# A causal convolution as 32x32 diagonal products, with the loop around it in a new order

## The chip, the cores and the metric

The kernel runs on one core of one Trainium2 chip. What counts is the device time of one execution in microseconds. Engines are named as in the profile: PE is TensorE (PEld its weight loads), DVE is VectorE, ACT is ScalarE, POOL is GpSimd, SP issues DMAs.

## What is computed

Causal linear attention with a decay per head, then a gated linear unit whose gate is a causal convolution of five taps, each channel by itself:

```python
# q, k, v: (8, 8, 576, 64); w_val, w_out: (512, 512); conv_w: (5, 512)
scores = q @ k.T / sqrt(64)
Dmat[h, i, j] = gamma[h] ** (i - j) if i >= j else 0
x = ((scores * Dmat) @ v).transpose(0, 2, 1, 3).reshape(8, 576, 512)
gate_pre[:, s, d] = sum(conv_w[t, d] * xp[:, s + t, d] for t in range(5))  # xp: x with 4 zero rows ahead
out = (sigmoid(gate_pre) * (x @ w_val)) @ w_out
```

## The kernel before

The sequence of each batch is cut into two units of 256 positions and a tail of 64. Sixteen full units come first (0 to 15); the tails of four batches make one unit each (16 and 17). The decay is factored: `gin` is multiplied into v, `gout` into the result, and a mask handles the diagonal blocks. What lies before a block of 128 comes in through a running state.

For one unit `n` these steps are issued, and every engine takes its own in the order in which they stand in the program (the schedule is written out by hand; the pools only say when a buffer is free):

- `load` issues the DMAs of k, q and v on SP's queue, five units ahead; `cast` makes bf16 of them on POOL (k, q, then v with the decay).
- `turn` transposes k and q on PE into the PSUM tile `a`; `take_turn` copies them, in two halves, to SBUF on ACT (`kq`, L249).
- `scores(n, 0)` and `scores(n, 1)` are 64x64 products into the PSUM tile `s` (L266), each half followed by `masks` on DVE (`p`, L276).
- `carried` multiplies the state into the output banks `o0` and `o1` (L307); `values` adds p times v there (L330).
- `take_x` brings the two output banks to SBUF as `xg`, the activations x, on DVE (L341; L348 for the tail).
- `update` makes the state's increment for the next unit in the tile `s` (L367); ACT copies it to `xf` (L375), and POOL adds it up (L380 to L392).
- `conv(n - 1, 0)` is the convolution of the unit before, as products with diagonal matrices `dg` (L424); `gates` takes the sigmoid on ACT (L433).
- `gate_values` multiplies x by w_val in two parts (L445), each followed by the product with the gate on DVE (`z`, L452).
- `rows_out` projects by w_out (L461), copies the two results on ACT (`ob`, L464) and stores them on SP's queue.

The eight PSUM banks are shared out to four pools of two banks each: `psa` (tile `a`: transposes, convolution), `pss` (tile `s`: scores and the state's update), `pso` (`o0`, `o1`) and `psv` (tile `v`: values of w_val and projections, two buffers of one bank). The tile `s` has one buffer, so scores wait until masks or `xf` have read what was there.

Before the loop the first four units are handled in a written-out lead-in, with loads and constants; the loop runs from unit 4 to 17. In it the order is: scores 0 and masks, convolution of n - 1, carried states woven into scores 1, masks, `gate_values`, `values`, `take_x`, `update(n + 1)`, `cast(n + 2)`, `turn(n + 1)`, `rows_out(n - 1)`. After the loop come the convolution, values and projections of unit 17.

In the convolution the channels of x stand in four blocks of 128 partitions. A 64x64 product takes one half of the partitions to one half of the output's, and a diagonal weight on 64 columns does one tap for 64 channels; four such products (two halves in, two halves out) go to two banks.

Of the kernel before, what the change touches and what calls it, by code (L numbers as in the profile page):

```python
# [13 lines left out]
F32 = mybir.dt.float32  # L14
BF16 = mybir.dt.bfloat16
AF = mybir.ActivationFunctionType
ALU = mybir.AluOpType
# [4 lines left out]
def kernel(  # L22
# [10 lines left out]
    nc = tc.nc  # L33
    B, H, S, D = q.shape
    DM = moe_w_val.shape[0]
    KC = moe_conv_w.shape[0]
    P = 128
    NP = H // 2
# [11 lines left out]
    consts = ctx.enter_context(tc.tile_pool(name="c", bufs=1))  # L50
# [5 lines left out]
    gp = ctx.enter_context(tc.tile_pool(name="gp", bufs=1))  # L56
    zp = ctx.enter_context(tc.tile_pool(name="zp", bufs=2))
# [3 lines left out]
    small = ctx.enter_context(tc.tile_pool(name="small", bufs=1))  # L61
    ps_a = ctx.enter_context(tc.tile_pool(name="psa", bufs=1, space=PSUM))
    ps_s = ctx.enter_context(tc.tile_pool(name="pss", bufs=1, space=PSUM))
    ps_o = ctx.enter_context(tc.tile_pool(name="pso", bufs=1, space=PSUM))
# [6 lines left out]
    NU = len(units)  # L71

    jobs = [(u,) for u in range(NU)]
    lo, hi = slice(0, 64), slice(64, 128)
# [3 lines left out]
    with tc.manual_schedule():  # L78
# [26 lines left out]
        wvf = consts.tile([P, NP, DM], F32, name="wvf")  # L105
        wof = consts.tile([P, NP, DM], F32, name="wof")
        load(1)
        nc.sync.dma_start(out=wvf, in_=moe_w_val.rearrange("(o i) n -> i o n", i=P))
        wo_src = moe_w_out.rearrange("(pr ab hl p) n -> ab hl p pr n", pr=2, ab=2, hl=2)
        for (p0, blk, ab, hl) in ((0, 0, 0, 0), (64, 0, 1, 0), (0, 2, 1, 1), (64, 2, 0, 1)):  # L110
            nc.sync.dma_start(out=wof[p0:p0 + 64, blk:blk + 2, :], in_=wo_src[ab, hl])
        for u in range(2, 5):
            load(u)

# [13 lines left out]
        nc.vector.tensor_copy(identf, ident[0:32, 0:32])  # L128
        id2 = small.tile([P, 64], F32, name="id2")
        nc.vector.tensor_tensor(id2, ident[:, 0:64], ident[:, 64:128], op=ALU.add)  # L130

        posi = small.tile([P, S], mybir.dt.int32, name="posi")
        for c in range(2 * NC2):
# [46 lines left out]

        wvb = consts.tile([P, NP, NP, P], BF16, name="wvb")
        wob = consts.tile([P, NP, DM], BF16, name="wob")
        dg = consts.tile([P, NP, KC, 64], BF16, name="dg")

        def prep_conv():
            cps = ps_a.tile([P, KC * NP], F32, name="a")
            nc.tensor.transpose(cps, cwn, identf[0:KC * NP, 0:KC * NP])
            cw = small.tile([P, KC * NP], F32, name="cw")
            nc.vector.tensor_copy(cw, cps)
            nc.vector.tensor_tensor(  # L190
                dg.rearrange("p o k j -> p k o j"),
                cw.rearrange("p (k o) -> p k o", o=NP).unsqueeze(3).to_broadcast([P, KC, NP, 64]),
                id2.unsqueeze(1).unsqueeze(1).to_broadcast([P, KC, NP, 64]), op=ALU.mult)

        def prep_wv():
            src = wvf.rearrange("p o (pr ab hl j) -> p o pr ab hl j", pr=2, ab=2, hl=2)
            for (i, (blk, j0, ab, hl)) in enumerate(((0, 0, 0, 0), (0, 64, 1, 0), (2, 0, 1, 1), (2, 64, 0, 1))):
                nc.scalar.copy(wvb[:, :, blk:blk + 2, j0:j0 + 64], src[:, :, :, ab, hl, :])

        def prep_wo():  # L200
            for o in range(NP):
# [29 lines left out]
        def turn(u, pool, parts=(0, 1)):  # L231

            if u not in kqt:
                kqt[u] = [tp_sb.tile([P, 2, 2, 2, 2, 64], BF16, name=f"kq{hf}") for hf in range(2)]
            if pool is ps_a:
                tps[u] = pool.tile([P, 2, 2, 2, 2, P], BF16, name="a")
            for i in parts:
                if pool is ps_a:
                    ps = tps[u][:, i]
                else:  # L240
                    ps = tps[u, i] = pool.tile([P, 2, 2, 2, P], BF16, name="v" if pool is ps_v else f"o{i}")
                for hf in range(2):
                    for prl in range(2):
                        for r in range(2):
                            h = 2 * (2 * hf + prl)
                            nc.tensor.transpose(ps[:, hf, prl, r, :], bf[u]["kq"[i]][:, r, h:h + 2, :].rearrange("p h d -> p (h d)"), ident)  # L246

        def take_turn(u, hf):
            nc.scalar.copy(kqt[u][hf].rearrange("p i l r c a -> p i (l r c a)"),  # L249
                           tps[u][:, :, hf].rearrange("p i l r a -> p i (l r a)"))  # L250
# [43 lines left out]
        def carried(u, odd, chs=(0, 1)):  # L294

            kind, b, cu = units[u]
            o = out_banks(u)
            for pr in range(NP):
                t = kqt[u][pr // 2]
                for c in chs:  # L300
                    par = c ^ odd
                    rows = half[par]
                    if kind == "full":
                        st = state.get((b, 2 * cu + c))
                        if st is None:
                            continue
                        nc.tensor.matmul(o[c][rows, pr, :], lhsT=st[rows, pr, :],  # L307
                                         rhs=t[rows, 1, pr % 2, :, c, :],
                                         start=first(u, c, par), stop=False, skip_group_check=True)
                    else:  # L310
                        for i in range(2):
                            st = state[b + 2 * c + i, 4]
                            cs = slice(i * 32, i * 32 + 32)
                            nc.tensor.matmul(o[c][rows, pr, :].rearrange("p (r a) -> p r a", r=2)[:, :, cs],
                                             lhsT=st[rows, pr, :], rhs=t[rows, 1, pr % 2, :, c, cs],
                                             start=first(u, c, par), stop=False, skip_group_check=True)
# [80 lines left out]
        def width(j):  # L397
            return W * len(jobs[j])

        def xs(j, rows, blk, shift):  # L400
            kind, b, c = units[jobs[j][0]]
            if kind == "full":
                c0 = c * W + shift
                return xg[rows, b, blk, c0:c0 + width(j)]
            c0 = NC2 * W + shift
            return xg[rows, b:b + GB * len(jobs[j]), blk, c0:c0 + TAIL]

        gsb, zsb = {}, {}
# [3 lines left out]
        def sets(j, i):  # L412
            return (0, 1) if len(jobs[j]) == 1 else (i,)
# [1 line left out]
        cps = {}  # L415

        def conv(j, i, gate=True):
            n, ss = width(j), sets(j, i)
            g = ps_a.tile([P, 2, len(ss), n], F32, name="a")
            for si, s in enumerate(ss):  # L420
                a, b = 2 * s, 2 * s + 1
                for kk in range(KC):
                    for (rows, blk, cols, bank) in ((lo, a, lo, 0), (hi, b, lo, 1), (lo, b, hi, 0), (hi, a, hi, 1)):
                        nc.tensor.matmul(g[cols, bank, si, :], lhsT=dg[rows, blk, kk, :], rhs=xs(j, rows, blk, kk),  # L424
                                         start=(si == 0 and kk == 0), stop=(si == len(ss) - 1 and kk == KC - 1),
                                         skip_group_check=True)
            cps[j, i] = g
            if gate:
                gates(j, i)

        def gates(j, i):
            t = gp.tile([P, 2, len(sets(j, i)), width(j)], F32, name="gate")
            nc.scalar.activation(t, cps[j, i], AF.Sigmoid)  # L433
            gsb[j, i] = t
            if i == 0:
                zsb[j] = zp.tile([P, NP, width(j)], BF16, name="z")

        vps = {}

# [9 lines left out]

        def gated(j, i, e):  # L450
            ss = sets(j, i)
            nc.vector.tensor_tensor(zsb[j][:, 2 * e + ss[0]:2 * e + ss[-1] + 1, :], gsb[j, i][:, e], vps[j, i, e], op=ALU.mult)  # L452

        outs = {}

# [22 lines left out]
        def gate_values(n, e):  # L478
            value(n, 0, e)
            gated(n, 0, e)  # L480

        def rows_out(n):
            project(n, 0, 0)
            project(n, 0, 1)
            store(n)
# [124 lines left out]
        for n in range(4, NU):  # L610
            if n + 5 < NU:
                load(n + 5)
            scores(n, 0)
            masks(n, 0)
            conv(n - 1, 0)
            carried(n, 0)
            scores(n, 1, lambda: carried(n, 1))
            masks(n, 1)
            for e in range(2):
                gate_values(n - 1, e)  # L620
            values(n, 1)
            values(n, 0)
            take_x(n)
            if n + 1 < NU:
                update(n + 1)
                if n + 2 < NU:
                    cast(n + 2)
                turn(n + 1, ps_a)
                take_turn(n + 1, 0)
                take_turn(n + 1, 1)  # L630
            rows_out(n - 1)
        conv(NU - 1, 0)
        for e in range(2):
            gate_values(NU - 1, e)
# [31 lines left out]
```

## Time and profile before

| | |
|---|---|
| two timed runs | 166.9 and 169.79 us, median 168.34 |
| span of the profiled execution | 169.3 us |
| mean granted TensorE clock | 0.969 |
| PE / DVE / ACT / POOL busy | 150.8 / 99.6 / 88.8 / 98.4 us |
| DMA | 40.35 MB, 238 GB/s in the mean |
| instruction queue of PE (q8) | 26 packets, 0.43 MB |

No other time of the profiled execution than its span is on record. In a group's line stand the source line, engine, operation, tiles written and read, shapes and count; then the busy time and the mean nanoseconds of one, and the engine's idle time before them with what ended it. In the chain and the timelines a line has a start and a length in microseconds from the start of the span.

### The profile page before, as it was taken

To read this page: it belongs to the slowest core of one execution; us is meant where nothing else is said; L and a number is where in the kernel's file an instruction comes from. 1 tells how busy PE (TensorE), PEld (TensorE's weight loads), DVE (VectorE), ACT (ScalarE), POOL (GpSimd) and SP (SyncE) were. 2 spreads that over 40 slices of the span, in tenths; PEclk is the share of its full clock that TensorE was granted. 3 is DMA by queue.
4 is the path that set the end of the run, shared out by engine and by line. 5 is a ranking of instruction groups with operands and counts; after the bars stand their busy time and mean duration, and the time that the engine had idled before them with its cause. 6 is when DMAs were issued, how large, how long until landed. Compare 5 with 4: busy or idle time off the path is not lost.

```text
span 169.3 us, 7640 instructions
## 1 busy us (share of the span) xinstructions
PE 150.8 (89%) x3384; PEld 112.8 (67%) x3402; DVE 99.6 (59%) x153; ACT 88.8 (52%) x127; POOL 98.4 (58%) x123
## 2 busy tenths in 40 slices
PE   6677589978899979998999999999999999999960
PEld 2366456647678756877787776868787877868620
DVE  5684543475758481858383856658584938668330
ACT  6965330565273827382838374564838382654520
POOL 7565197157875846584849594956769499100000
PEclk9999755999999999999999999999999999999999
DMA  4999978999999999999999999787980311303125
GB/s 143 290 341 351 284 218 258 316 325 322 314 323 329 282 342 295 307 332 323 329 282 327 296 304 274 251 235 237 240 273 21 128 68 60 127 9 128 45 78 126
DMA packets 61071, 40.35 MB, mean 238 GB/s; under 512 B 2394, under 2 KB 57710, under 8 KB 61038
## 3 DMA queue, kind: packets, MB, share of 16 engines
q1 hardware_dynamic: 61008, 39.86, 77.7%
q8 instruction: 26, 0.43, 1.1%
q14 instruction: 7, 0.06, 0.1%
q10 hardware_dynamic: 30, 0.01, 0.0%
HBM read 30.42 MB, written 9.44 MB: 235 GB/s over the span
## 4 chain that ended last, share of the span: by engine, by line
PE 77%; DMA 5%; DVE 4%; issue 4%; POOL 4%; ACT 2%; SPq 1%; POOLq 0%; ACTq 0%; DVEq 0%
PE v L445 18%; PE v L461 17%; PE a L424 13%; PE a L246 8%; PE s L266 6%; PE o L330 6%; PE o L307 3%; DMA fqc<-in_q_dram 3%; PE s L367 2%; POOL vb L215 2%; DMA fkc<-in_k_dram 2%; DVE p L276 2%; SPq L90 1%; PE o L246 1%; DVE z L452 1%
## 5 line engine op out<-in xcount | busy, mean ns | idle before, releaser
L276 DVE TENSOR_TENSOR p<-s,mask 128x1024 bf16<-128x1024 f32 x28 | 34.3, 1224 | 40.2 <-PE s L266 40.2
L445 PE MATMUL v<-xg,wvb 128*128 128x256 bf16 x288 | 36.6, 281 | 0.5 <-DVE xg L341 0.5
L215 POOL TENSOR_TENSOR vb<-fvc,gin 128x1024 bf16<-128x1024 f32 x18 | 34.3, 1903 | 3.3 <-DMA fvc<-in_v_dram 3.3
L461 PE MATMUL v<-wob,z 128*128 128x512 bf16 x126 | 33.5, 380 | 1.3 <-DVE z L452 0.4
L249 ACT COPY kq<-a 128x1024 bf16<-128x1024 bf16 x28 | 27.0, 1015 | 10.0 <-PE a L246 10.0
L445 PEld LDWEIGHTS <-wvb 128*128 128x128 bf16 x288 | 27.3, 100 | 6.4 <-issue 1.4
L452 DVE TENSOR_TENSOR z<-gate,v 128x512 bf16<-128x512 f32 x36 | 24.6, 683 | 9.2 <-ACT gate L433 5.3
L433 ACT ACTIVATE gate<-a 128x1024 f32<-128x1024 f32 x18 | 18.4, 1024 | 16.1 <-PE a L424 9.1
L464 ACT COPY ob<-v 128x512 f32<-128x512 f32 x36 | 20.0, 605 | 9.6 <-PE v L461 9.6
L424 PE MATMUL a<-xg,dg 64*64 64x256 bf16 x720 | 24.2, 278 | 0.0
L375 ACT COPY xf<-s 128x512 f32<-128x512 f32 x12 | 7.0, 586 | 31.2 <-PE s L367 31.2
L341 DVE TENSOR_TENSOR xg<-o,gout 128x512 bf16<-128x512 f32 x32 | 22.2, 741 | 0.2
L461 PEld LDWEIGHTS <-z 128*128 128x128 bf16 x144 | 13.0, 98 | 13.6 <-DVE z L452 1.4
L424 PEld LDWEIGHTS <-dg 64*64 64x64 bf16 x720 | 20.5, 109 | 2.1 <-DVE xg L348 0.4
L266 PEld LDWEIGHTS <-kq 64*64 64x64 bf16 x576 | 13.5, 106 | 11.0 <-issue 10.0
L266 PE MATMUL s<-kq 64*64 64x128 bf16 x512 | 16.5, 223 | 3.2 <-issue 2.8
L389 POOL TENSOR_TENSOR mid<-run,xf 128x256 f32<-128x256 f32 x8 | 5.8, 727 | 20.3 <-ACT xf L375 14.2
L221 POOL CAST kb<-fkc 128x1024 bf16<-128x1024 f32 x16 | 16.6, 1039 | 0.2 <-DMA fkc<-in_k_dram 0.2
L221 POOL CAST qb<-fqc 128x1024 bf16<-128x1024 f32 x15 | 15.6, 1041 | 0.2 <-DMA fqc<-in_q_dram 0.2
L380 POOL CAST s<-xf 128x256 bf16<-128x256 f32 x8 | 3.2, 398 | 20.2 <-ACT xf L375 13.6
L330 PE MATMUL o<-p,vb 64*64 64x128 bf16 x576 | 12.6, 224 | 1.2 <-DVE p L276 1.2
L330 PEld LDWEIGHTS <-vb 64*64 64x64 bf16 x576 | 9.4, 109 | 5.3 <-issue 5.1
(75 smaller groups left out, 157.7 us busy)
## 6 DMA issues: line engine op xcount, KB each, us to landing
fkc<-in_k_dram SPq DMA_DIRECT2D x32, 256.0 KB, 5.1
fqc<-in_q_dram SPq DMA_DIRECT2D x32, 256.0 KB, 5.1
fvc<-in_v_dram SPq DMA_DIRECT2D x32, 256.0 KB, 5.1
out_dram<-ob SPq DMA_DIRECT2D x16, 512.0 KB, 4.8
wvf<-in_moe_w_val_dram SPq DMA_DIRECT2D x1, 1024.0 KB, 9.2
wof<-in_moe_w_out_dram SPq DMA_DIRECT2D x4, 256.0 KB, 10.0
fkc<-in_k_dram SPq DMA_DIRECT2D x8, 128.0 KB, 4.1
fqc<-in_q_dram SPq DMA_DIRECT2D x8, 128.0 KB, 4.5
```

The lines of the kernel that those rows point to most:

```text
L215: nc.gpsimd.tensor_tensor(t.rearrange("p h r d -> p (h r) d"), loaded["v", u].rearrange("p h (r d) -> p (h r) d", r=2), gin[:, units[u][2] ...
L221: (eng or nc.gpsimd.tensor_copy)(t.rearrange("p r h d -> p h r d"), loaded[n, u].rearrange("p h (r d) -> p h r d", r=2))
L249: nc.scalar.copy(kqt[u][hf].rearrange("p i l r c a -> p i (l r c a)"), tps[u][:, :, hf].rearrange("p i l r a -> p i (l r a)"))
L266: nc.tensor.matmul(s[half[c], par, prl, r, :], lhsT=t[half[par], 0, prl, r, c, :], rhs=t[half[par], 1, prl, :, c, :], start=True, stop=Tru ...
L276: nc.vector.tensor_tensor(p.rearrange("p e l r a -> p (e l) (r a)"), sps[u, hf].rearrange("p e l r a -> p (e l) (r a)"), m.rearrange("p r ...
L330: nc.tensor.matmul(o[c][half[par], pr, :], lhsT=vb[half[c], 2 * pr + par, r, :], rhs=p[half[c], par, prl, r, :], start=first(u, c, par), s ...
L341: nc.vector.tensor_tensor(x[:, b, :, PAD + i0:PAD + i0 + P].rearrange("p o (a r) -> p o r a", r=2), o[c].rearrange("p o (r a) -> p o r a", ...
L424: nc.tensor.matmul(g[cols, bank, si, :], lhsT=dg[rows, blk, kk, :], rhs=xs(j, rows, blk, kk), start=(si == 0 and kk == 0), stop=(si == len ...
L445: nc.tensor.matmul(vp[:, si, :], lhsT=wvb[:, o, 2 * e + s, :], rhs=xs(j, slice(0, P), o, PAD), start=(si == 0 and o == 0), stop=(si == len ...
L452: nc.vector.tensor_tensor(zsb[j][:, 2 * e + ss[0]:2 * e + ss[-1] + 1, :], gsb[j, i][:, e], vps[j, i, e], op=ALU.mult)
L461: nc.tensor.matmul(o, lhsT=z[:, r, :], rhs=wob[:, jj, :], start=(jj == 0), stop=(jj == NP - 1))
L464: (eng or nc.scalar.copy)(outs[u][:, r], o)
```

## The change

Three things. The convolution uses products of 32x32: sixteen per tap (four quarters of the partitions in, four quarters out), one bank for each quarter in, so that it takes four banks, the two of `a` and the two of `o0` and `o1`. The sigmoid is taken bank by bank. So that x's channels meet the right gate, the columns of w_val and the rows of w_out are laid out in another order. And the loop has `gate_values` right after the convolution, and `turn(n + 1)` and `rows_out(n - 1)` before `values`, `take_x`, `update` and `cast`.

```diff
-        wo_src = moe_w_out.rearrange("(pr ab hl p) n -> ab hl p pr n", pr=2, ab=2, hl=2)
-        for (p0, blk, ab, hl) in ((0, 0, 0, 0), (64, 0, 1, 0), (0, 2, 1, 1), (64, 2, 0, 1)):
-            nc.sync.dma_start(out=wof[p0:p0 + 64, blk:blk + 2, :], in_=wo_src[ab, hl])
+        wo_src = moe_w_out.rearrange("(j i p) n -> j p i n", j=4, i=4)
+        for j in range(4):
+            nc.sync.dma_start(out=wof[32 * j:32 * j + 32], in_=wo_src[j])
...
+        id4 = small.tile([P, 32], F32, name="id4")
+        nc.vector.tensor_tensor(id4, id2[:, 0:32], id2[:, 32:64], op=ALU.add)
...
-        dg = consts.tile([P, NP, KC, 64], BF16, name="dg")
+        dg = consts.tile([P, NP, KC, 32], BF16, name="dg")
...
-            src = wvf.rearrange("p o (pr ab hl j) -> p o pr ab hl j", pr=2, ab=2, hl=2)
-            for (i, (blk, j0, ab, hl)) in enumerate(((0, 0, 0, 0), (0, 64, 1, 0), (2, 0, 1, 1), (2, 64, 0, 1))):
-                nc.scalar.copy(wvb[:, :, blk:blk + 2, j0:j0 + 64], src[:, :, :, ab, hl, :])
+            src = wvf.rearrange("p o (j i c) -> p o j i c", j=4, i=4)
+            for i in range(4):
+                nc.scalar.copy(wvb[:, :, i].rearrange("p o (j c) -> p o j c", j=4), src[:, :, :, i, :])
...
         def conv(j, i, gate=True):
-            n, ss = width(j), sets(j, i)
-            g = ps_a.tile([P, 2, len(ss), n], F32, name="a")
-            for si, s in enumerate(ss):
-                a, b = 2 * s, 2 * s + 1
-                for kk in range(KC):
-                    for (rows, blk, cols, bank) in ((lo, a, lo, 0), (hi, b, lo, 1), (lo, b, hi, 0), (hi, a, hi, 1)):
-                        nc.tensor.matmul(g[cols, bank, si, :], lhsT=dg[rows, blk, kk, :], rhs=xs(j, rows, blk, kk),
-                                         start=(si == 0 and kk == 0), stop=(si == len(ss) - 1 and kk == KC - 1),
-                                         skip_group_check=True)
-            cps[j, i] = g
-            if gate:
-                gates(j, i)
+            n = width(j)
+            g = ps_a.tile([P, 2, 512], F32, name="a")
+            go = [ps_o.tile([P, 512], F32, name=f"o{c}") for c in range(2)]
+            bank = [g[:, 0], g[:, 1], go[0], go[1]]
+            for kk in range(KC):
+                for d in range(4):
+                    for rg in range(4):
+                        cg = (rg + d) % 4
+                        rows, cols = slice(32 * rg, 32 * rg + 32), slice(32 * cg, 32 * cg + 32)
+                        nc.tensor.matmul(bank[rg][cols, 0:n], lhsT=dg[rows, cg, kk, :], rhs=xs(j, rows, cg, kk),
+                                         start=(kk == 0), stop=(kk == KC - 1), skip_group_check=True)
+            cps[j, i] = (g, go)
+            gates(j, i)
...
-            t = gp.tile([P, 2, len(sets(j, i)), width(j)], F32, name="gate")
-            nc.scalar.activation(t, cps[j, i], AF.Sigmoid)
+            n = width(j)
+            t = gp.tile([P, NP, n], F32, name="gate")
+            g, go = cps[j, i]
+            for c in range(2):
+                nc.scalar.activation(t[:, 2 + c], go[c][:, 0:n], AF.Sigmoid)
+            nc.scalar.activation(t[:, 0:2], g[:, :, 0:n], AF.Sigmoid)
...
             conv(n - 1, 0)
+            for e in range(2):
+                gate_values(n - 1, e)
             carried(n, 0)
             scores(n, 1, lambda: carried(n, 1))
             masks(n, 1)
-            for e in range(2):
-                gate_values(n - 1, e)
+            if n + 1 < NU:
+                turn(n + 1, ps_a)
+                take_turn(n + 1, 0)
+                take_turn(n + 1, 1)
+            rows_out(n - 1)
             values(n, 1)
             values(n, 0)
             take_x(n)
...
                 update(n + 1)
                 if n + 2 < NU:
                     cast(n + 2)
-                turn(n + 1, ps_a)
-                take_turn(n + 1, 0)
-                take_turn(n + 1, 1)
-            rows_out(n - 1)
```

More of the change, by code (lines that the diff above doesn't have):

```diff
@@ L191, in prep_conv @@
                 dg.rearrange("p o k j -> p k o j"),
-                cw.rearrange("p (k o) -> p k o", o=NP).unsqueeze(3).to_broadcast([P, KC, NP, 64]),
-                id2.unsqueeze(1).unsqueeze(1).to_broadcast([P, KC, NP, 64]), op=ALU.mult)
+                cw.rearrange("p (k o) -> p k o", o=NP).unsqueeze(3).to_broadcast([P, KC, NP, 32]),
+                id4.unsqueeze(1).unsqueeze(1).to_broadcast([P, KC, NP, 32]), op=ALU.mult)
         def prep_wv():
-            src = wvf.rearrange("p o (pr ab hl j) -> p o pr ab hl j", pr=2, ab=2, hl=2)
-            for (i, (blk, j0, ab, hl)) in enumerate(((0, 0, 0, 0), (0, 64, 1, 0), (2, 0, 1, 1), (2, 64, 0, 1))):
-                nc.scalar.copy(wvb[:, :, blk:blk + 2, j0:j0 + 64], src[:, :, :, ab, hl, :])
+            src = wvf.rearrange("p o (j i c) -> p o j i c", j=4, i=4)
+            for i in range(4):
+                nc.scalar.copy(wvb[:, :, i].rearrange("p o (j c) -> p o j c", j=4), src[:, :, :, i, :])
         def prep_wo():
@@ L417, in conv @@
         def conv(j, i, gate=True):
-            n, ss = width(j), sets(j, i)
-            g = ps_a.tile([P, 2, len(ss), n], F32, name="a")
-            for si, s in enumerate(ss):
-                a, b = 2 * s, 2 * s + 1
-                for kk in range(KC):
-                    for (rows, blk, cols, bank) in ((lo, a, lo, 0), (hi, b, lo, 1), (lo, b, hi, 0), (hi, a, hi, 1)):
-                        nc.tensor.matmul(g[cols, bank, si, :], lhsT=dg[rows, blk, kk, :], rhs=xs(j, rows, blk, kk),
-                                         start=(si == 0 and kk == 0), stop=(si == len(ss) - 1 and kk == KC - 1),
-                                         skip_group_check=True)
-            cps[j, i] = g
-            if gate:
-                gates(j, i)
-        def gates(j, i):
-            t = gp.tile([P, 2, len(sets(j, i)), width(j)], F32, name="gate")
-            nc.scalar.activation(t, cps[j, i], AF.Sigmoid)
+            n = width(j)
[11 more added lines that the diff above has]
+            gates(j, i)
+        def gates(j, i):
+            n = width(j)
[4 more added lines that the diff above has]
+            nc.scalar.activation(t[:, 0:2], g[:, :, 0:n], AF.Sigmoid)
             gsb[j, i] = t
-            if i == 0:
-                zsb[j] = zp.tile([P, NP, width(j)], BF16, name="z")
+            zsb[j] = zp.tile([P, NP, n], BF16, name="z")
         vps = {}
@@ L451, in gated @@
             ss = sets(j, i)
-            nc.vector.tensor_tensor(zsb[j][:, 2 * e + ss[0]:2 * e + ss[-1] + 1, :], gsb[j, i][:, e], vps[j, i, e], op=ALU.mult)
+            nc.vector.tensor_tensor(zsb[j][:, 2 * e + ss[0]:2 * e + ss[-1] + 1, :], gsb[j, i][:, 2 * e:2 * e + 2], vps[j, i, e], op=ALU.mult)
         outs = {}
```

## The prediction

> **What bounds the kernel now.** I read the page's busy line and its chain first, then the chain in order of time for one turn of the loop, then the groups, and last ScalarE's timeline of the same turn.
>
> ```profile
> PE 150.8 (89%) x3384; PEld 112.8 (67%) x3402; DVE 99.6 (59%) x153; ACT 88.8 (52%) x127; POOL 98.4 (58%) x123
> PE 77%; DMA 5%; DVE 4%; issue 4%; POOL 4%; ACT 2%; SPq 1%; POOLq 0%; ACTq 0%; DVEq 0%
> ```
>
> TensorE is the bound on average. In the loop it is so with no gap at all (start, length, what):
>
> ```profile
> 98.34 0.35 PE s L266 x16
> 98.69 1.23 PE a L424 x40
> 99.92 0.22 PE o L307 x4
> ...
> 100.62 1.85 PE v L445 x16
> 102.48 0.57 PE o L330 x32
> 103.05 0.28 PE s L367 x32
> 103.33 1.00 PE a L246 x16
> ```
>
> With the projections after it (0.22 + 0.05 + 1.46 = 1.73) and 0.70 for carried states and second scores between 99.92 and 100.62, a turn is 0.35 + 1.23 + 0.70 + 1.85 + 0.57 + 0.28 + 1.00 + 1.73 = 7.71 us, all PE. From 49.70 (scores of unit 4) to 161.63 (end of the last value) it takes 111.93 us. The groups give the durations needed (busy, mean ns, idle before):
>
> ```profile
> L249 ACT COPY kq<-a 128x1024 bf16<-128x1024 bf16 x28 | 27.0, 1015 | 10.0 <-PE a L246 10.0
> L464 ACT COPY ob<-v 128x512 f32<-128x512 f32 x36 | 20.0, 605 | 9.6 <-PE v L461 9.6
> L375 ACT COPY xf<-s 128x512 f32<-128x512 f32 x12 | 7.0, 586 | 31.2 <-PE s L367 31.2
> L341 DVE TENSOR_TENSOR xg<-o,gout 128x512 bf16<-128x512 f32 x32 | 22.2, 741 | 0.2
> ```
>
> The order on ScalarE in a turn (start, length; the bracket is idle time before):
>
> ```profile
> 103.47 0.59 ACT L375 COPY xf<-s 128x512 f32<-128x512 f32 x1 [2.43 <-PE s L367]
> 104.36 1.93 ACT L249 COPY kq<-a 128x1024 bf16<-128x1024 bf16 x2 [0.30 <-PE a L246]
> 106.18 1.09 ACT L464 COPY ob<-v 128x512 f32<-128x512 f32 x2
> 107.73 1.02 ACT L433 ACTIVATE gate<-a 128x1024 f32<-128x1024 f32 x1 [0.46 <-ACT ob L464]
> ```
>
> The state copy (xf) comes first and finds ScalarE idle; PE meanwhile has transposes and projections, 2.73 us, before the next scores need the two banks that xf reads. That is the cover which the new order removes.
>
> The chain has two pieces named issue in the loop, and one before it:
>
> ```profile
> 15.71 2.83 issue
> ...
> 62.29 1.47 issue
> ...
> 79.43 0.48 issue
> ```
>
> PE stops there in the midst of like instructions (at 62.29 inside one state update). The trace's DMA records explain it: the instruction queue (26 packets of 16,384 bytes on the page) started packets at 16.01, 61.41 and 77.57, and PE resumed 2.53, 2.35 and 2.34 us after each start. PE's entries (weight loads and matmuls) before the stops number 448, 2236 and 3002: 1788 and 766 apart, 7x256 and 3x256 but for a few missing records. So a packet is 256 entries, is asked for while the block before it runs, and is usable about 2.35 us after its start. Counted from the first entry of the block before, it is usable after 4.1 us in the mean for the 13 blocks from 44 to 110 us (1.9 to 5.8) and 3.2 us later, when the loads are over. A block is executed in 4.1 to 7.0 us now, so only two of the loop were late, 1.95 us together.
>
> **The change, part by part.** *Products.* Forty 64x64 products become eighty 32x32 ones. The trace of before has no 32x32 product. With 64x64 it shows rounds of four starting 109.6 ns apart at 256 columns: ten rounds 1.10, and 0.13 to enter. Sixteen at once would be five rounds, 0.55; no more than eight at once 1.10; four at once twenty rounds, 2.20. A round needs 32 entries in 110 ns; inside a round the trace has entries 1.7 ns apart, 54 ns, and the two-streams-from-the-same-rows case of 64x64 runs at full rate. I take 0.55, with 0.13 to enter and 0.1 for one more change of array shape per turn (64x64 scores to 128x128 values took 149 ns from last start to first): 0.78 in place of 1.23, 0.45 saved in a turn.
>
> The Trainium skill's page "TensorE: Matmul & The Clock Gate" (Part 3, measured speedup) gives 10.6 times for sixteen tiles of 512 columns; by that my estimate for eighty products of 0.11 us each would be 0.83 plus entry, and the sum some 4 us higher.
>
> *Gates.* One sigmoid of 1024 columns (1024 ns) becomes two of 256 and one of 512. ScalarE's copies of these sizes take 374 and 605 ns: 1.35 us, 0.33 more. They lie under the value products (1.85). The carried products now wait for the first two (0.2 + 0.75 after the convolution), also under the values. Hidden in the loop; not hidden in the lead-in.
>
> *The other preparation.* Four loads of the output weights of the same 256 KB, four casts of equal size, one more small DVE add (0.2) and diagonals of half the size (1.49 to 0.75): they balance, and lie under the first loads. Nothing.
>
> *The order.* On PE the new turn is scores, convolution, values products (1.85), carried and second scores (0.70), transposes (1.00), projections (1.73), p-times-v (0.57), update (0.28). On ScalarE: gates, two kq copies, two ob copies, then xf. Scores of the next unit wait for xf, because both use the same two banks. From the end T of the transposes: kq starts at T + 0.03, the four copies take 2.91 (104.36 to 107.27), xf half a microsecond more (0.59 less the overlap of records): xf ends at T + 3.44. PE is through the update at T + 2.58 and would be free; it waits 0.94 with the signal. Even with an idle ScalarE it would wait about 0.8 (0.14 to xf's start, 0.59, 0.08). Period: 0.08 + 0.35 + 0.78 + 1.85 + 0.70 + 1.00 + 3.44 = 8.20, 0.49 more than now. The second wait, of the convolution for the two xg products (1.38 after p-times-v, 0.2 to start, 0.07), ends at 1.65 and lies under xf (0.86 + 0.94 after p-times-v, then scores). VectorE (5.0 of 8.2) keeps up. GpSimd has 1.85 of state work and 2.05 of k and q casts after xf, and the transposes come 3.7 after xf: level to 0.2 us.
>
> Without instruction waits: first transposes end at 4.7, first xf at 8.1, ten periods to 90.1. Unit 15 ends its p-times-v 7.1 later, at 97.2. Units 16, 17 and the last convolution have no xf; there xg is what the convolution waits for (1.65, then 2.0 with the tail's four products of 448 ns): 8.3, 7.7 and 4.7 more: 117.9. Now, without the 1.95, it is 110.0. So the order costs 7.9 net of what the products save.
>
> *Instructions.* A turn goes from 384 to 464 entries, and 320 of them (p-times-v 64, update 64, scores 32, convolution 160) now stand together, in 0.57 + 0.28 + 0.94 + 0.35 + 0.78 = 2.9 us. A block that begins between p-times-v and the update (about one in six) is executed in 2.3 to 2.7 us; one that begins in the update's end, the scores or the start of the convolution (one in five) in 3.4 to 4.0; the others in 5 to 6. Against 4.1 us the first are late by 1.6, the second by some 0.6 (delays vary), the rest not. Of 25 blocks, two thirds while loads run: 2.8 x 1.6 + 3.4 x 0.6 = 6.5; one third at 3.2 us: about 1. I take 7.5, ends 2 (as now) and 11: 5.5 more than now.
>
> The Trainium skill's page "Runtime: NRT & Kernel Launch" (Instruction fetch mechanics) calls the crossing of a 16 KiB boundary mostly hidden. The rows above show three that were not.
>
> *Lead-in.* The stop at entry 448 now falls inside the first convolution. After it come the rest of that convolution (0.4), 0.2 and two gates (0.75) before the carried products (0.25): scores of unit 1 start 1.6 later. Later waits of that stretch are for loads and casts and may swallow it or add a further late block: minus 1 to plus 3.5; I take 1.6.
>
> Sum: 169.3 + 7.9 - 1.95 + 7.5 + 1.6 = 184.35, taken as 184. The span of 169.3 lies within the two timed runs (166.9 to 169.79, median 168.34), and I make no correction.
>
> **The rivals.** *Instruction blocks stay hidden.* For it: the mean turn lengthens too, and PE's own waits give packets time. Against it: the three stops above. Then 184 - 5.5 = 178.5, and with the lead-in swallowed 176. This stays slower.
>
> *The small products don't run sixteen at once.* No row excludes it. Eight at once: 0.55 more in each of 14 convolutions, 7.7, less some 2 of instruction waits: 190. Four at once: 1.65 each, 23, less 5: 202.
>
> The Trainium skill's page "TensorE: Matmul & The Clock Gate" (Wait — 56ns, not 53.3ns?) has matmuls start no closer than about 25 ns, which would make eighty 2.0 us and lead to about the same time; but L367 starts 32 in 0.28 us here, 8.8 ns each, so the trace disagrees.
>
> *The other side: the wait for xf vanishes.* If the scores found their banks free by the time PE gets there, for instance because the copies ahead of xf overlap more than their rows show, the turn would be 7.71 - 0.45 = 7.26: 14 x 0.45 = 6.3 less, 163, or 167 with half of the instruction waits. It decides where the wait per turn is below 0.25 us (3.4 us over 14 turns is the 2%). Against it: xf alone, from its trigger to its signal, is 0.8.
>
> *A draw.* Wait about equal to the saving and blocks hidden: 166 to 172.
>
> **How the numbers follow.** Forecast (slower, order and instructions both): 0.55. Blocks hidden, still slower: 0.16. Fewer than sixteen at once: 0.14. Draw: 0.07. Other side: 0.08. So faster by over 2% 0.08, within 2% (about what a measurement of this kernel can tell from no change) 0.07, slower 0.85. The range goes from 173, below the hidden-blocks case, to 196, beyond eight at once with instruction waits at their high end.
>
> **What would show it.** Right: on PE's waits, scores waiting for the xf copy about 0.9 us in each of eleven turns; xf directly behind ob on ScalarE; a convolution of 0.6 to 0.8 us; issue pieces of 5 to 10 us in the chain, at p-times-v, update, scores or convolution. Wrong: a turn below 7.7 us, a convolution of 1.1 us or more, or issue pieces no larger than now.

## The result, and the profile after

The changed kernel takes 188.03 us in the median of two runs (186.93 and 189.12); the ratio to the kernel before is 1.128 (95% interval 1.112 to 1.144). It is slower, by about 20 us; the prediction was 184, range 173 to 196. Executions of one kernel differ by a few per cent: each ratio here is taken over the undisturbed ones alone, while medians and ranges are over all. The profiled execution has a span of 187.4 us, 18.1 more than before. Line numbers are shifted: scores L268, convolution L429, values L451, projections L467, update L369, xf L377, kq L251, ob L470, gates L439 and L440.

The busy line, the instruction queue and the chain by engine, from the page after:

```profile
PE 149.1 (80%) x4104; PEld 105.4 (56%) x4122; DVE 100.0 (53%) x154; ACT 90.1 (48%) x163; POOL 96.6 (52%) x123
q8 instruction: 32, 0.52, 1.1%
PE 12%; DVE 3%; issue 1%; ACT 1%
```

PE is about as long busy as before (150.8), and idle for 38 us in place of 18.5. Six more instruction packets were fetched. The chain's shares are small because it reaches back only to 151.7 us here; the loop must be read from waits and timelines.

PE's waits (engine, what it waited for: total, times, longest):

```profile
PE s L268 <- ACT xf L377: 10.0, 11, 0.9
PE o L429 <- issue: 3.8, 1, 3.8
PE a L429 <- DVE xg L350: 3.0, 2, 1.6
PE a L429 <- issue: 3.0, 3, 1.5
```

The first is the forecast wait, eleven times 0.91 us. The 3.8 on issue is in the lead-in; the three that make 3.0 us are in convolutions of the loop. ScalarE in one turn, and PE's scores in the same turn:

```profile
104.16 1.93 ACT L251 COPY kq<-a 128x1024 bf16<-128x1024 bf16 x2 [2.67 <-PE a L248]
105.97 1.10 ACT L470 COPY ob<-v 128x512 f32<-128x512 f32 x2
106.92 0.63 ACT L377 COPY xf<-s 128x512 f32<-128x512 f32 x1
```

```profile
105.78 0.64 PE L332 MATMUL o<-p,vb 64*64 64x128 bf16 x32
106.25 0.45 PE L369 MATMUL s<-vb,kb 64*64 64x64 bf16 x32
107.60 0.42 PE L268 MATMUL s<-kq 64*64 64x128 bf16 x16 [0.91 <-ACT xf L377]
```

ScalarE has no gap between kq, ob and xf; PE has done the update by 106.7 and stands until xf is over, at 107.55.

From the scores of unit 4 to the end of the last value products the loop takes 126.6 us (53.2 to 179.9) against 112.0 before (49.6 to 161.6). Turns without a late instruction block are 8.3 and 8.5 us apart (7.71 and 7.74 before). In five places PE stops inside the loop with no wait named: at 54.27, 66.64, 82.02, 111.14 and 134.75, 5.8 us together beyond the ordinary spacing (a sixth stop, at 101.40, is 0.2 us). It resumes 2.3 to 2.5 us after the start of a packet of the instruction queue, and 3.05 us after the one that took longest to move (1.75 us, from 109.14).

### The profile page after: what moved, and what is told of

It is laid out like the page before. It is cut to its first block, busy times and chain, and to the rows that moved or that the text cites. A ratio compares the mean times of both kernels' runs of the same rounds, so it can differ in the third digit from the quotient of the medians.

```text
span 187.4 us, 9094 instructions
## 1 busy us (share of the span) xinstructions
PE 149.1 (80%) x4104; PEld 105.4 (56%) x4122; DVE 100.0 (53%) x154; ACT 90.1 (48%) x163; POOL 96.6 (52%) x123
## 5 line engine op out<-in xcount | busy, mean ns | idle before, releaser
L251 ACT COPY kq<-a 128x1024 bf16<-128x1024 bf16 x28 | 27.0, 1016 | 33.5 <-PE a L248 33.5
L458 DVE TENSOR_TENSOR z<-gate,v 128x512 bf16<-128x512 f32 x36 | 23.9, 687 | 25.6 <-ACT gate L440 21.7
L451 PE MATMUL v<-xg,wvb 128*128 128x256 bf16 x288 | 36.8, 281 | 0.6 <-DVE xg L343 0.5
L467 PE MATMUL v<-wob,z 128*128 128x512 bf16 x126 | 33.5, 380 | 1.5 <-DVE z L458 0.5
L439 ACT ACTIVATE gate<-o 128x256 f32<-128x256 f32 x36 | 11.9, 382 | 41.4 <-issue 25.8
L451 PEld LDWEIGHTS <-wvb 128*128 128x128 bf16 x288 | 27.2, 100 | 7.0 <-issue 1.3
L268 PE MATMUL s<-kq 64*64 64x128 bf16 x512 | 18.3, 224 | 11.2 <-ACT xf L377 10.0
L429 PE MATMUL a<-xg,dg 32*32 32x256 bf16 x720 | 19.6, 282 | 7.3 <-DVE xg L350 3.0
L470 ACT COPY ob<-v 128x512 f32<-128x512 f32 x36 | 20.0, 607 | 8.9 <-PE v L467 8.9
L429 PE MATMUL o<-xg,dg 32*32 32x256 bf16 x720 | 19.6, 283 | 4.4 <-issue 3.8
L429 PEld LDWEIGHTS <-dg 32*32 32x32 bf16 x1440 | 13.7, 88 | 16.6 <-issue 9.6
L268 PEld LDWEIGHTS <-kq 64*64 64x64 bf16 x576 | 14.7, 108 | 14.1 <-issue 13.4
L467 PEld LDWEIGHTS <-z 128*128 128x128 bf16 x144 | 13.0, 98 | 13.7 <-DVE z L458 1.4
L382 POOL CAST s<-xf 128x256 bf16<-128x256 f32 x8 | 3.2, 397 | 25.1 <-ACT xf L377 18.5
```

The lines of the kernel that those rows point to most:

```text
L268: nc.tensor.matmul(s[half[c], par, prl, r, :], lhsT=t[half[par], 0, prl, r, c, :], rhs=t[half[par], 1, prl, :, c, :], start=True, stop=Tru ...
L429: nc.tensor.matmul(bank[rg][cols, 0:n], lhsT=dg[rows, cg, kk, :], rhs=xs(j, rows, cg, kk), start=(kk == 0), stop=(kk == KC - 1), skip_grou ...
L451: nc.tensor.matmul(vp[:, si, :], lhsT=wvb[:, o, 2 * e + s, :], rhs=xs(j, slice(0, P), o, PAD), start=(si == 0 and o == 0), stop=(si == len ...
L467: nc.tensor.matmul(o, lhsT=z[:, r, :], rhs=wob[:, jj, :], start=(jj == 0), stop=(jj == NP - 1))
L470: (eng or nc.scalar.copy)(outs[u][:, r], o)
```

## The experiments

**The order alone.** The kernel before with the loop's new order, products unchanged:

```diff
             conv(n - 1, 0)
+            for e in range(2):
+                gate_values(n - 1, e)
             carried(n, 0)
             scores(n, 1, lambda: carried(n, 1))
             masks(n, 1)
-            for e in range(2):
-                gate_values(n - 1, e)
+            if n + 1 < NU:
+                turn(n + 1, ps_a)
+                take_turn(n + 1, 0)
+                take_turn(n + 1, 1)
+            rows_out(n - 1)
```

(and the same steps taken out behind `take_x` and `update`)

> The kernel before with the new order of the loop alone: its 64x64 products, its gates and its lead-in stay. Theory: the order itself costs time, since scores wait for the state copy, which is now last in ScalarE's queue. A turn is then 0.08 + 0.35 + 1.23 + 1.85 + 0.70 + 1.00 + 3.44 = 8.65 us against 7.71, and the whole 183 to 186 us. Rival: the small products and the 40% more weight loads and matmuls are what costs; then this kernel takes 168 to 172 us.

Measured: 182.3 us in the median (179.7 to 185.2), ratio 1.068 (1.056 to 1.081). Most turns are 8.70 and 8.51 us apart in the trace, 8.60 in the mean where 8.65 was expected, and the wait is there:

```profile
PE s L266 <- ACT xf L375: 11.6, 11, 2.5
```

The longest holds something else as well: ScalarE's copy ob was itself held up, by a store of the output.

```profile
65.30 1.07 ACT L464 COPY ob<-v 128x512 f32<-128x512 f32 x2 [1.50 <-DMA out_dram<-ob]
```

After that wait the granted clock was 0.5 for 3.4 us (66.97 to 70.39), so that this turn and the next took 10.3 and 10.1 us. The order by itself costs about 0.9 us a turn without one 32x32 product. The rival is out as the whole cause. The two runs on which the ratio rests took 179.7 and 180.3 us, 3 us under the 183 that was expected.

**The products alone.** The changed kernel with the old order of the loop (the edit above in reverse):

> The 32x32 products in four banks, the new gates and the channel order, with the loop in its old order. Theory: the carried products stand right behind the convolution and want the two output banks back, so that they wait for two gates, 0.2 + 0.75 + 0.07 = 1.0 us a turn, with nothing to cover it; the convolution gives 0.29 back. 14 turns make +10, late instruction blocks +2 to +5, the lead-in +3.5: 183 to 188 us. Rival: the order is the whole of the loss and the products by themselves are a gain; then 163 to 169 us.

Measured: 184.4 us, ratio 1.091 (1.070 to 1.113). The wait for the gates was expected at 1.0 us a turn; it is there, but smaller, 0.65 us in the mean:

```profile
PE o L309 <- ACT gate L439: 8.4, 13, 0.8
```

The products by themselves are no gain either. The two halves of the change are not additive: each alone takes 11 to 15 us, both take 20. The new order covers the wait for the gates and opens the one for xf.

**The update in other banks.**

```diff
-                update(n + 1)
+                update(n + 1, own=True)
```

> The changed kernel with the state's update written into the two value banks (v) in place of the scores' banks, so that scores no longer wait for the copy of the state. Theory: the order took away two covers at once, and the other wait takes over: the convolution wants xg, which is ready 1.65 us after the last p-times-v, while PE gets there 0.63 us after it. The wait for the copy, 0.91 in each of eleven turns, becomes a wait of about 1.0 for VectorE: 185 to 189 us. Rival: the wait for the copy is the loss; then 10 us less, 177 to 179.

Measured: 189.1 to 194.2 us, median 192.6, where 185 to 189 was expected; the profiled execution is the shortest of the four, span 187.3 against 187.4. So there is no gain, the rival is out, and the time lies at the upper end of the theory's range or above it. The mechanism is another one. Of the waits of PE:

```profile
PE v L369 <- ACT ob L470: 5.3, 22, 0.3
...
PE a L429 <- DVE xg L350: 3.0, 2, 1.6
...
PE a L429 <- DVE xg L343: 1.3, 1, 1.3
```

The update now waits for its own banks, since the projections' results are still in them and ScalarE copies them behind kq: two gaps of 0.42 and 0.49 us between PE's starts in every turn. Where that wait ends, xg is nearly ready (in one turn it is over at 124.98, and the convolution starts at 125.04), and xg holds up PE only in turns with no update, as in the changed kernel. Taking away the wait for xf left the turns without a late block at 8.2 to 8.5 us, because ScalarE's queue of four copies stands behind both. What PE would do with neither wait, this run does not show.

**Without the loads of units 8 to 15.**

```diff
             src = SRC[n]
+            if u >= 8 and kind == "full":
+                loaded[n, u] = loaded[n, u - 4]
+                return
```

> The changed kernel without the loads of units 8 to 15 (they use the k, q and v that are already in the four buffers), so that the DMA engines are nearly idle from about 60 us on. It leaves those loads out. Theory: the stops named issue in the loop are late instruction packets, and they are late because the packets stand behind loads; with the loads gone most of the 3.7 us of stops after 60 us go: 183 to 186 us, packets usable 3.2 us after the start of the block before them. Rival: the stops belong to the dense code and not to the loads, or are no packets at all: 187 to 189 us and as many stops.

Measured: 185.6 us in the median (183.6 to 192.8), ratio 1.090 (1.078 to 1.103). In the profiled execution, which took 192.8, there is no stop without a named wait from 61 to 133 us, where the changed kernel had three (2.8 us). Between 66 and 123 us the packets start 0.6 us after the block before them in the mean; in the changed kernel it is 1.7 for the same blocks. Two stops of 2.6 us stand at 56 and 136 us, while loads run (the last are those of the tails). After each of them the granted clock was 0.5 for 3.4 us (59.60 to 63.02, 138.11 to 141.52), and the two turns took 12.5 us in place of 8.3 to 8.5: the stop itself and about 1.5 us more. That is part of why this execution is long although it has fewer stops. The median fits the theory, with a spread as wide as the effect.

**The covers given back.** In the changed kernel the first projection stays ahead of p-times-v, its copy on VectorE, and the second goes behind the update:

```diff
-            rows_out(n - 1)
+            project(n - 1, 0, 0, dve)
             values(n, 1)
             values(n, 0)
             take_x(n)
...
                     cast(n + 2)
+            project(n - 1, 0, 1)
+            store(n - 1)
```

> The changed kernel with its products and its early values, but with the covers given back: the first projection stays between the transposes and p-times-v (its copy goes to VectorE), the second moves behind the update, ahead of the next scores. Theory: PE then has 0.86 us to do while the state is copied and xg is made; the wait for xf goes, and about 0.15 us of waiting for xg stays. A turn is 0.35 + 0.94 + 1.85 + 0.70 + 1.00 + 1.73 + 0.57 + 0.28 + 0.15 = 7.57 us before late instruction blocks; with those (3 to 5 more than before) and the lead-in (3.5) 174 to 178 us. Rival: the small products themselves disturb the turn; then it stays at 183 to 187.

Measured: 181.1 us, ratio 1.079 (1.067 to 1.092). The wait for xf is gone, and turns between full units, less their stops, are 7.4 to 7.6 us (7.57 expected). But the stops grew, and they stand at the head of PE's waits:

```profile
PE a L429 <- issue: 4.7, 7, 1.0
PE o L429 <- issue: 2.9, 1, 2.9
PE o L332 <- issue: 2.5, 1, 2.5
```

The single ones of 2.9 and 2.5 are in the lead-in; in the loop the gaps add up to about 8.5 us, and the loop starts only at 54.5. So the miss against 174 to 178 is in the instruction blocks (5 to 7 us were expected in the loop) and in a lead-in that ends 4.9 us later than before (3.5 expected). Every stop in the loop before 132 us falls where the count of PE's entries reaches a multiple of 256 from the first stop's 449, so what PE stands for there are packets.

**The same order with the 64x64 products.**

> The same order of the loop with the 64x64 products of before. Theory: a turn of 7.57 + 0.29 = 7.86 us against 7.71, lead-in and instruction blocks as before: 169 to 173 us, faster than the 32x32 products in the same order in spite of their shorter convolution. Rival: with the waits out of the way the small products win, and this one is 2 us or more slower than they are.

Measured: 170.8 to 175.4 us, profiled span 170.4; the kernel before, measured beside it, took 165.6 to 169.2, median 167.5. There is no ratio with an interval; the two lowest runs, 170.8 and 172.1, are some 2.6% above the six lowest of the kernel before. Turns are 7.67 and 7.87 us apart, and the loop of the trace is nearly neutral, 112.6 us against 112.0; where the rest of the difference lies is not shown. The old products beat the small ones in this order by 9 us of span (170.4 against 179.4). The profiled loops take 112.6 and 117.2; the rest is the lead-in, 50.2 and 54.5. A turn without a stop is shorter with the small products (7.4 to 7.6), so in the loop it is the late blocks that make them the slower ones.

**More entries, nothing else.** The kernel before, with forty products of zeros over 16 columns added to each convolution of the loop:

```diff
+                        if j >= 3:
+                            z = xs(j, rows, blk, kk)
+                            z = z[:, 0:16] if len(z.shape) == 2 else z[:, 0, 0:16]
+                            nc.tensor.matmul(g[cols, bank, si, 0:16], lhsT=zero[rows, 0:64], rhs=z,
+                                             start=False, stop=(si == len(ss) - 1 and kk == KC - 1), skip_group_check=True)
```

> The kernel before, with forty more products in each convolution of the loop (zeros over 16 columns, added to what is there), so that PE has the changed kernel's 464 entries a turn in the old order, with nothing else changed. Their array time is about 0.1 to 0.15 us a turn, 2 us in all. Theory: the entries themselves cost, since packets come in late: another 2 to 5 us, 171 to 176 in all, and three or more stops named issue in the loop. Rival: packets keep up in the old order, and only the array time shows: 168 to 171, no more than two stops.

Measured: 178.0 us, ratio 1.067 (1.057 to 1.077), 2 us above the range. Turns without a stop grew by 0.1 to 0.3 us, some 3 us in all where 2 were expected. The rest is stops, 8.5 us from start to start in the loop, where the kernel before has 2.3; the longer ones in the chain (start, length):

```profile
48.24 1.65 issue
73.74 1.55 issue
79.51 0.61 issue
84.73 1.46 issue
99.44 0.65 issue
```

At all nine stops of the loop PE's entries before them number 449, the count at its first stop, plus a whole number of 256s (1729, 1985, 2753, 3009 and so on to 4545). This kernel has the old order, the old products, no new wait, and little more work. It loses as much as the new order alone does.

**The same without the loads of units 8 to 15.** The edit is that of the fourth experiment:

> The kernel with forty more products a turn in the old order, now without the loads of units 8 to 15 (left out; the four buffers are used again). Theory: the stops named issue are packets held up behind loads; of the stops after 60 us, about 6 us in the run with all loads, at least 4 go: 171 to 174 us. Rival: 464 entries a turn are too many for the packets with or without loads: 176 to 179 us and as many stops.

Measured: 172.0 us, ratio 1.027 (1.020 to 1.034). The chain's issue pieces in the loop are down to two longer ones (and two under half a microsecond):

```profile
58.38 0.86 issue
117.38 1.01 issue
```

The entries are the same 464 a turn. Between 61 and 111 us a packet starts 2.7 us after the block before it in the run with all loads, in the mean, and 1.0 us in this one. The granted clock is 1.0 through the loop of both traces, so it is not the clock that differs. Packets mostly keep up when the DMA engines are quiet, and often don't while loads run. This is the cleanest evidence for the cause of the stops.

**Half the columns.** Each 32x32 product of the loop over 128 columns in place of 256 (half of the convolution is left out):

```diff
+                        m = n if j < 3 else n // 2
...
-                        nc.tensor.matmul(bank[rg][cols, 0:n], ...
+                        nc.tensor.matmul(bank[rg][cols, 0:m], ...
```

> The changed kernel with each 32x32 product of the loop over half of its columns (the gate of the first half is used for both, so half of the convolution is left out). In the changed kernel's trace eighty products take 0.73 us from first to last start, and after the first 32 they follow 8.3 ns apart, in turn with their weight loads. Theory: that pace is the issue of 160 instructions, and with 128 columns the convolution takes 0.6 to 0.7 us all the same. Rival: the array sets the pace, and it falls to 0.35 to 0.45 us.

Measured, one run: 188.2 us. From first to last start an undisturbed convolution takes 0.64 us with 128 columns and 0.73 with 256. From the third round on products start 8.3 to 8.4 ns apart in both kernels. Half the array's work saves an eighth, so the columns do not set the pace; a product and its weight load in 8.3 ns fits the issue of instructions, some 4.1 ns each.

**Fewer warm-up products.** The kernel before, with 9 wide warm-up products in place of 32 narrow ones in its lead-in:

```diff
-        warm(6, 128)
+        warm(2, 384)
...
-        warm(8, 128)
+        warm(2, 512)
...
-        warm(5, 128, ps_s)
+        warm(1, 512, ps_s)
```

> The kernel before with fewer entries in its lead-in: 32 warm-up products of 128 columns become 9 of 384 or 512, so that the first block of instructions reaches 46 entries further and the stop of 2.83 us comes after the scores of unit 1 and not before them. Theory: VectorE's masks and what follows start up to 1.5 us earlier; as later waits for loads and casts take up part of it, 166 to 168 us where the kernel before takes 167.5, ratio 0.99 to 1.0. Rival: those later waits swallow it all, or the next block is late instead: 1.0 to 1.01.

Measured: ratio 0.990 (0.984 to 0.997), but it rests on three of twelve runs, and the plain medians are 169.0 and, for the kernel before, 168.4. I take it as undecided. The stop moved as meant, to 16.35 in the trace, 2.1 us long. No version here is shown to beat the kernel before.

## Why the prediction was right, step by step

The direction, the two mechanisms and the time, within its range, were right. Three terms of the sum were off, by about +2.5, +2.0 and -1.7 us; that they partly cancelled is luck, and the sum is 3 us short of the span.

- *The wait for xf*: 0.94 us a turn forecast, 0.91 measured, eleven times. The first experiment shows that the order by itself makes it, the fifth that giving back the cover takes it away. The statement that xg lies just under it was right too: in the turn shown above xg is over at 107.83 and the convolution starts at 107.95. With the update elsewhere PE still stood, for a third reason which the prediction had not named, the value banks.
- *The convolution*: the term that failed. Forecast at 0.78 us, five rounds of 110 ns with entry and one change of shape. Measured: 0.73 from first to last start and 0.21 from the last start to the first value product, 0.94. The first 32 products do start in two rounds about 120 ns apart; then each product and each weight load take their turn, 8.3 ns for the pair. "Entries 1.7 ns apart, 54 ns a round" was read within a burst of 32 entries and taken for a rate that lasts. The 0.21 is not the price of the small shape, as the forecast's 0.1 for a change of shape has it: the kernel with the order alone, with 64x64 products of 256 columns, has 0.20 there, and the one with 32x32 products of 128 columns 0.155. So a turn is 8.3 to 8.5 us and not 8.20, about 2.5 us over the loop.
- *The saving* in a turn, forecast at 0.45, is 0.29 (1.23 against 0.94); from whole turns it is 0.21 (8.60 with the order alone, 8.39 here).
- *Instruction blocks*: 7.5 us forecast in the loop, 5.8 measured in this execution. The theory holds in four kernels: entries without order (+10.5 us, most of it stops), the same without loads (few stops left), the covers given back (stops grow to 8.5), loads left out of the changed kernel. The short blocks counted for less, and the packets' late starts for more, than the forecast had it: of three blocks of 2.4 to 2.6 us only the one that ends at 134.75 had a late packet behind it, and the other four stops end blocks of 3.4 to 4.5 us whose next packet had started 1.4 to 3.4 us after them. So the closeness of 7.5 and 5.8 is partly luck. It would also follow that a late block costs nothing while PE stands for xf; the larger stops with the covers given back fit that, but no run tests it alone. The page "Runtime: NRT & Kernel Launch" of the Trainium skill (Instruction fetch mechanics) calls this cost mostly hidden. Most of the 32 packets do cost nothing here, but seven come clearly late.
- *Lead-in*: 1.6 us forecast, 3.6 measured against the kernel before. Scores of unit 1 start 1.5 us later (20.00 against 18.54), which is the step that the forecast had. The scores of unit 2 are 2.9 us later, and the loop 3.6. Two of the added parts have a place in the trace: a second late block (PE stops for 1.7 us at 23.52), and the convolution of unit 2, which waits 0.8 us at 42.84 until kq is copied out of the output banks that it now needs. Beside them the granted clock differs: it is 0.5 for 13.65 us here (18.09 to 31.74) and for 10.24 us before (18.86 to 29.10). The rows of the two pages, the kernel before first (40 slices of the span):

```profile
PEclk9999755999999999999999999999999999999999
PEclk9999556999999999999999999999999999999997
```

Across kernels the loop starts at 46.4 to 50.2 us with 64x64 products (six profiles) and at 51.7 to 55.1 with 32x32 (six), 4.8 apart in the mean; the lead-ins of the second group also had more time at a clock of 0.5, 10.2 to 17.1 us against 0 to 10.2. How much of the difference is instruction blocks and how much the clock stays open.

- *Sum*: 184.35, plus some 2.5 for convolution and turn, plus 2 for the lead-in, less 1.7 for blocks: 187.2, where the span is 187.4. The forecast took a span for a time; the time of the profiled run is 1.7 us above its span (189.12 and 187.4), so as a time the sum reads 186.
- *Rivals*: that instruction blocks stay hidden fell with the kernel that has more entries and nothing else. That fewer than sixteen run at once came in a mild form: the first two rounds are sixteen wide, and after them, with starts 8.3 ns apart, about thirteen products of 0.11 us overlap. The Trainium skill's page "TensorE: Matmul & The Clock Gate" (Part 3, measured speedup) led to an estimate of 0.83 us for eighty products. The run has 0.73 from first to last start and, with the last product's 0.11, 0.84: the trace agrees, and the 0.55 that the sum used is what failed. Its 25 ns floor between starts (Wait — 56ns, not 53.3ns?) is not what tiles show here, at 8.3 ns.

## What to carry to other kernels

Splitting products to fill an idle array saved 0.29 us of the 0.45 hoped for in a turn, since starting the products took longer than running them, and the count of instructions has a second price: count entries per turn against the packets that bring them, above all while loads run. When steps in a gap-free loop are moved, look at each shared buffer and ask which engine's queue empties it and what now stands ahead of that copy; removing the wait that the profile names may only show the next one behind the same queue.

## What was not expected of the hardware

- PE starts the first 32 entries of a convolution 1.7 ns apart, and from the third round on it takes about 4.1 ns for each: eighty 32x32 products with their weight loads take 0.73 us over 256 columns and 0.64 over 128.
- The time from the last start of a convolution to the first 128x128 product follows the columns and hardly the shape: 208 ns for 32x32 over 256 columns, 201 for 64x64 over 256, 155 for 32x32 over 128.
- Forty nearly empty products a turn cost 6.7% with all loads, and 2.7% without those of units 8 to 15, from packets of 16 KB that mostly take 0.9 us to move and are usable some 2.35 us after their start.
- Three stops of PE of 2.6 to 2.7 us in loops, two for packets and one for xf, were each followed by a granted clock of 0.5 for 3.4 us, and the turns concerned lost about 1.5 us more. Shorter stops in the loops, up to 2.2 us, were not, but for one of 1.3 us with the products alone.
